# Sigmoid attention and a split-float16 feed-forward on one core: four decoded weight groups used by two batches, a third batch's attention in float32, and one sigmoid over two PSUM banks

## The chip, the cores and the metric

The kernel runs on one core of one Trainium2 chip. The time is the device time of one execution in microseconds (us). The kernel before took 1580.22 us, the median of three runs (1577.51 to 1587.48). A core has a matrix engine (TensorE, PE in the profile; its weight loads are PEld), a vector engine (VectorE, DVE), an activation engine (ScalarE, ACT), GpSimd (POOL), and a queue that here issues every DMA (SyncE, SP). Working memory is SBUF; matrix products land in PSUM, eight banks of 512 float32 numbers per partition.

## The reference

```python
def _attn_ref(q, k, v):                       # q, k, v: (8 batches, 12 heads, 448, 64), float32
    scores = scale * np.matmul(q, k.transpose(0, 1, 3, 2)) - np.log(S)
    attn = 1.0 / (1.0 + np.exp(-scores))
    return np.matmul(attn, v).astype(np.float32)

def _moe_ref(x, U, V, w_ch1, w_ch2):          # x: attention, heads side by side, (8, 448, 768)
    xt = x.transpose(0, 2, 1)
    h = xt @ U @ V                            # rank 32 over the 448 positions
    u = x + h.transpose(0, 2, 1)
    ch = np.maximum(u @ w_ch1, 0.0) @ w_ch2   # 768 -> 3072 -> 768
    return (u + ch).astype(np.float32)
```

U, V, w_ch1 and w_ch2 are float64; q, k and v are float32.

## The kernel before

Everything of a batch is kept with its 768 channels on partitions: six blocks of 128 channels by 448 positions, called u (`ua`, `ub` with a number in the profile). The heads go in six pairs.

**Attention** (`pair`, line 518). For batches 0 and 1 (`b < WHOLE`, WHOLE = 2) the scores and the products with the values are float32 matmuls straight from the loaded q, k and v (lines 495, 506, 510). For batches 2 to 7 each operand is scaled and split into a float16 high and a float16 low part, and three float16 products stand for one float32 product. This needs, for each pair, the largest magnitudes of q, k and v (`bound` on ACT, line 415), a scale through a DMA round trip (`scale_by_dma`), the high parts on POOL and the low parts on DVE, and the same split of the sigmoids (ACT line 603, DVE line 362, function `rest`). A pair has four blocks of key positions, of 128, 128, 128 and 64 (block 3 comes first); the two heads of a block go to two PSUM banks and are read by two sigmoids of 448 elements a partition each (line 582), eight in a pair.

**Mixing** (`mix`, `mix_half`): the rank-32 product over positions, added to u. Batches 1 to 7 are then parked in DRAM. For batches 0 to 3 `u_parts` splits u into float16 parts `us` (tiles us__86 and us__87).

**Feed-forward, batches 0 to 3** (`ffn_in`, line 830, `ffn_out`, line 850). The 3072 hidden channels come in six groups of 512. A group is 4 chains of 18 matmuls (768 inputs, three split products) and 6 chains of 12 matmuls: 144 matmuls of 128x448, float16. Each chain into the hidden layer is read by two ACT relus and one DVE subtraction (lines 837 to 839), each chain out of it is added to u on DVE (line 857; shown as line 362).

**Decoding** (`decode`, line 772). While batch 0 runs, each group's two weight matrices are loaded as raw float64 words (`w<-w_in`), in four pieces of 768 columns each. A piece takes three integer operations on DVE (`to_f32`: one on line 359, two on line 362), the largest magnitude on ACT (line 415), then, once the scale of all four pieces has gone through a small PE transpose (line 377), the high part on ACT and the low part on DVE (line 362). The finished pair goes to a two-deep ring (`w__88` to `w__91`) and to DRAM (`scratch`). Batches 1 to 3 load each group again from `scratch` (`fetch`).

**Batches 4 to 7** run the feed-forward in pairs of batches with seven block products in place of eight (`in_quad`, `out_quad`; all their matmuls are line 1025), after sums of weight quarters (`quarter_sums`) and of u blocks (`far_forms`, `near_forms`) have been formed.

**Order.** Nothing is ordered by a scheduler on the chip or by the framework: each operation is recorded in `Plan` with a rough cost and a position (`pos`), and a list scheduler in the kernel file walks the engines, takes the operation that can start first, the lowest position among several, and so fixes one instruction order for each engine. Positions come from the table of numbers on lines 59 to 67 (START, BEFORE, PREP and so on). On the chip each engine then works its list in that order, and an instruction that waits holds up everything behind it on its engine. The feed-forward slots of batches 0 to 3 are 24, `slots = [(b, g) for b in range(PLAIN) for g in range(NG)]` (line 1145): six groups of batch 0, six of batch 1, and so on; the attention of batch 1 is placed among batch 0's slots, that of batches 2 to 7 (in the order `LATER`) among the slots of batches 1 to 3.

Of the kernel before, what the change touches and what calls it, by code (L numbers as in the profile page):

```python
# [37 lines left out]
P = 128  # L38
D = 64
# [25 lines left out]
U_AT, U_STEP = 4.779, 5.064
LEAD, SUMS, STEP_K, STEP_I, FFN_LEAD = 28.26, 19.594, 38.128, 13.566, 4.0
# [22 lines left out]
class Plan:  # L89
# [36 lines left out]
    def order(self):  # L126
# [19 lines left out]
        def room(i):  # L146

            when, taken = 0.0, []
            for t in self.ops[i][7]:
                if t.got is None:  # L150
# [3 lines left out]
                    for b in t.buffers:  # L154
                        if b.live or b in taken or any(x.live for x in b.shares):
# [65 lines left out]
def fused_kernel(ctx: ExitStack, tc: tile.TileContext, q, k, v, wu, wv, w1, w2, out):  # L221
# [20 lines left out]
    puv = buf("puv", [1], F32)  # L242
# [12 lines left out]
    a_, at_ = buf("a", [14 * S], F32), buf("at", [5 * S], F32)  # L255
    A2, A1 = [Buffer(a_[:, 2 * i * S : 2 * (i + 1) * S]) for i in range(6)], [Buffer(a_[:, i * S : (i + 1) * S]) for i in (12, 13)]
# [39 lines left out]
    BANK = [Buffer(ps.tile([P, 512], F32, name=f"bank{i}")) for i in range(8)]  # L296
# [29 lines left out]
    FAR = {n: [Buffer(dram.tile([P, n], F32, name=f"far{n}_{i}")) for i in range(3)] for n in (3,)}  # L326
# [95 lines left out]

    FFN = 6 * (4 * 18 + 6 * 12) * MM
    BEGIN = [START]
    for b in range(PLAIN):
        BEGIN.append(BEGIN[-1] + FFN + (ROOM0 if not b else ROOM * len(LATER) / (PLAIN - 1)))

# [50 lines left out]
    def scores_of(b, js, products, kp, pos, early):  # L478


        sc = {(j, h): plan.tile("sc", BANK if early else PS_[b], False) for j in js for h in range(2)}
        n = 1 if b < WHOLE else 3

        def fn():
            for j in js:
                for i, (x, y) in enumerate(products()):
                    for h in range(2):
                        if b < WHOLE:
                            o = sc[j, h].x[:, :S] if j < 3 else sc[j, h].x[rows_of(h), :S]
                            keys = x[rows_of(h), j * P : min(S, j * P + P)]  # L490
                        else:
                            o = sc[j, h].x[:, :S]
                            first = j * P - (D if j == 3 and h else 0)
                            keys = x[rows_of(h), first : first + P]
                        nc.tensor.matmul(o, keys, y[rows_of(h)], start=i == 0, stop=i == n - 1)  # L495

        scored.append(pe(len(js) * (4 if b < WHOLE else 3) * MM + 0.2, fn, kp, list(sc.values()), pos, after=values_ops[-2:-1]))
        return sc

    def values_of(b, products, tiles, kp, pos):  # L500
# [14 lines left out]
        values_ops.append(pe((16 if b < WHOLE else 12) * MM + 0.2, fn, kp, [av], pos))  # L515
        return av

    def pair(b, p, at, d):
        whole = b < WHOLE
# [16 lines left out]
        else:  # L536
            prep = at - PREP
            st, ss = plan.tile("stg", STG), sm("ss", 3)
            for i in range(2):
                bound(lambda i=i: qk.x[:, i, :], S, lambda i=i: ss.x[:, i : i + 1], kqk[2 * i : 2 * i + 2], (ss, i), prep - BOUNDS, 0.73)  # L540
            bound(lambda: v32.x.rearrange("p a b -> p (a b)"), 512, lambda: ss.x[:, 2:3], [v32], (ss, 2), prep - BOUNDS, 0.82)
            s, inv = scale_by_dma(ss, [(ss, i) for i in range(3)], 3, "qkv", prep - BOUNDS + 1)
            cc, cv = sm("c", 1), sm("cv", 1)
            pool(0.5, lambda: ts(nc.gpsimd, cc.x, inv.x[:, 0:1], inv.x[:, 1:2], ALU.mult, 1.0 / math.sqrt(D), ALU.mult), [inv], [cc], prep + 1)
            pool(0.45, lambda: ts(nc.gpsimd, cv.x, inv.x[:, 2:3], 1.0 / A_UP, ALU.mult, 1.0, ALU.mult), [inv], [cv], prep + 1)
# [14 lines left out]
            pool(0.8, lambda: scaled(part(4), v32.x, s.x[:, 2:3]), [v32, s], [(st, 4)], prep + 6, plan.wrote["decoded"])  # L560
            dve2(0.75, lambda: rest(part(5), v32.x, s.x[:, 2:3], part(4)), [v32, s, (st, 4)], [(st, 5)], prep + 7)
# [17 lines left out]
            c, kc = cc, [cc]  # L579

        def sigmoid(cost, out_, in_, rows, pos, kin, kout):
            act(cost, lambda: nc.scalar.activation(  # L582
                out_(), in_(), AF.Sigmoid, bias=bias_s[rows], scale=c if whole else c.x[rows]), kin + ["bias"] + kc, kout, pos)

        sc = {}
        for n, j in enumerate((3, 0, 1, 2)):
# [6 lines left out]
            to = a if whole else plan.tile(*(("t1", AT1) if j == 3 else ("t2", AT2)))  # L593
# [692 lines left out]
```

## Time and profile before

| what | value |
|---|---|
| median of 3 runs | 1580.22 us |
| lowest and highest run | 1577.51, 1587.48 us |
| span of the profiled execution | 1577.4 us |
| busy PE, DVE, ACT, POOL | 98%, 71%, 54%, 23% |
| PE's first matmul after the span's start | 4.2 us |
| first feed-forward matmul | 83.7 us |
| mean granted TensorE clock | 0.996 |

The profiled execution's span, 1577.4 us, lies 0.1 us under the lowest of the three runs, and 2.8 us under their median. A row of a timeline has the start, the busy time, the engine, the line, the operation with output and inputs, their shapes, and the number of instructions merged into it; in brackets stand the idle time before it and what ended that. A matmul is pipelined, so its row's busy time is longer than its place in the stream: the price of a run of matmuls is read from its start to the next row's start. A float32 matmul appears as two records. In a row of windows stand, for each engine, busy time and number of instructions, then the granted clock (PEclk), the DMA share and GB/s.

### The profile page before, as it was taken

Reading aid. Unit: us, or ns where it says so; the run is one execution under the profiler, and the core shown is the slowest. Engines: PE = TensorE matmul, PEld = TensorE weight load, DVE = VectorE, ACT = ScalarE, POOL = GpSimd, SP = SyncE. Lnnn points to the kernel's source line nnn. Section 1 sums busy time; section 2 is a strip of 40 time slices with the busy share of each in tenths; the row PEclk is TensorE's granted clock in tenths of the full one; section 3 lists DMA queues with packets and bytes.
Section 4 is the critical chain, followed back from the end, with each engine's and each line's share of the span. In section 5 each row is a group of like instructions: output and inputs, shape, how many; then the busy total and the mean of one; then the engine's idle time right before and its main releaser. Section 6 shows DMA issues by size and latency. Waiting matters only on the chain.

```text
span 1577.4 us, 23653 instructions
## 1 busy us (share of the span) xinstructions
PE 1551.6 (98%) x8711; PEld 763.4 (48%) x8711; DVE 1125.1 (71%) x1886; ACT 854.6 (54%) x1521; POOL 355.7 (23%) x465
## 2 busy tenths in 40 slices
PE   8999989999999999999999999999999999999999
PEld 3344444544444444444444454455555555555554
DVE  3898889757776867667666777578768677565656
ACT  6756655468867766867867758342323524121210
POOL 0200002452212344211163410044554310000000
PEclk9999999999999999999999999999999999999999
DMA  8788988886576887664765684987576664233321
GB/s 250 249 296 275 295 276 259 301 237 162 148 215 162 196 255 230 189 184 131 199 189 173 189 246 156 283 268 230 182 222 204 242 209 165 105 106 137 109 106 70
DMA packets 208723, 319.36 MB, mean 202 GB/s; under 512 B 126176, under 2 KB 174688, under 8 KB 196320
## 3 DMA queue, kind: packets, MB, share of 16 engines
q1 hardware_dynamic: 208608, 317.86, 64.6%
q8 instruction: 68, 1.11, 0.3%
q14 instruction: 47, 0.39, 0.1%
HBM read 246.25 MB, written 77.42 MB: 205 GB/s over the span
## 4 chain that ended last, share of the span: by engine, by line
PE 93%; DMA 2%; DVE 2%; ACT 1%; SPq 1%; issue 0%; ACTq 0%; DVEq 0%
PE bank L1025 36%; PE bank L830 20%; PE bank L850 19%; PE bank L495 8%; PE bank L510 6%; PE bank L506 2%; DMA qk__100<-k_in 1%; PE bank L747 1%; DMA qk__98<-q_in 0%; PE bank L756 0%; PE bank L666 0%; SPq L339 0%; DVE stg__107 L362 0%; PE bank L654 0%; PE bank L691 0%
## 5 line engine op out<-in xcount | busy, mean ns | idle before, releaser
L850 PE MATMUL bank<-h__92,w__90 128*128 128x448 f16 x864 | 172.7, 353 | 0.8 <-DVE ua__76 L362 0.8
L850 PE MATMUL bank<-h__93,w__91 128*128 128x448 f16 x864 | 170.7, 353 | 0.4 <-DVE e_w__187 L380 0.4
L362 DVE SCALAR_TENSOR_TENSOR a<-at,a 128x896 f16<-128x896 f32 (+1 forms) x144 | 145.2, 1020 | 27.7 <-ACT a L603 26.9
L830 PEld LDWEIGHTS <-w__88 128*128 128x128 f16 x864 | 84.1, 98 | 86.4 <-issue 11.3
L830 PEld LDWEIGHTS <-w__89 128*128 128x128 f16 x864 | 83.8, 99 | 86.7 <-issue 13.2
L850 PEld LDWEIGHTS <-w__90 128*128 128x128 f16 x864 | 81.7, 98 | 87.0 <-issue 14.3
L603 ACT ACTIVATE a<-at 128x896 f16<-128x896 f32 (+1 forms) x144 | 122.9, 854 | 0.7
L850 PEld LDWEIGHTS <-w__91 128*128 128x128 f16 x864 | 82.5, 98 | 83.9 <-issue 10.4
L1025 PEld LDWEIGHTS <-w__88 128*128 128x128 f16 x756 | 73.8, 98 | 72.8 <-issue 4.1
L1025 PEld LDWEIGHTS <-w__90 128*128 128x128 f16 x756 | 74.0, 98 | 69.0
L1025 PEld LDWEIGHTS <-w__91 128*128 128x128 f16 x756 | 74.0, 98 | 68.9
L1025 PEld LDWEIGHTS <-w__89 128*128 128x128 f16 x756 | 74.0, 98 | 68.9
L913 POOL TENSOR_TENSOR w<-w 128x384 f32<-128x384 f32 x96 | 103.8, 1082 | 5.0
L830 PE MATMUL bank<-us__86,w__89 128*128 128x448 f16 x432 | 86.6, 357 | 4.0 <-DVE ua__79 L362 3.4
L830 PE MATMUL bank<-us__86,w__88 128*128 128x448 f16 x432 | 85.7, 357 | 3.7 <-DVE ua__74 L362 3.7
L830 PE MATMUL bank<-us__87,w__88 128*128 128x448 f16 x432 | 85.5, 353 | 0.3 <-ACT r__94 L837 0.3
L830 PE MATMUL bank<-us__87,w__89 128*128 128x448 f16 x432 | 85.8, 353 | 0.0
L582 ACT ACTIVATE at<-bank,bias_s,c__223 128x448 f32<-128x448 f32 (+1 forms) x96 | 66.5, 722 | 21.3 <-PE bank L495 17.2
L909 POOL TENSOR_TENSOR w<-w 128x384 f32<-128x384 f16 x48 | 45.6, 974 | 119.1 <-DVE xnt L917 76.5
L582 ACT ACTIVATE at<-bank,bias_s,c__222 128x448 f32<-128x448 f32 (+1 forms) x96 | 66.8, 721 | 8.2 <-PE bank L495 6.3
L582 ACT ACTIVATE at<-bank,bias_s,c__221 128x448 f32<-128x448 f32 (+1 forms) x96 | 66.9, 722 | 7.1 <-PE bank L495 6.4
L909 POOL TENSOR_TENSOR w<-w__88 128x384 f32<-128x384 f16 x16 | 14.9, 952 | 209.2 <-DVE stg__108 L362 185.8
(1195 smaller groups left out, 3097.7 us busy)
## 6 DMA issues: line engine op xcount, KB each, us to landing
w<-w_in SPq DMA_DIRECT2D x48, 768.0 KB, 6.0
forms<-xnt SPq DMA_DIRECT2D x24, 768.0 KB, 4.3
w__88<-forms SPq DMA_DIRECT2D x12, 1344.0 KB, 5.7
w__89<-forms SPq DMA_DIRECT2D x12, 1344.0 KB, 5.8
w__90<-forms SPq DMA_DIRECT2D x12, 1344.0 KB, 6.0
w__91<-forms SPq DMA_DIRECT2D x12, 1344.0 KB, 6.1
forms<-scratch SPq DMA_DIRECT2D x144, 96.0 KB, 4.2
w__88<-scratch SPq DMA_DIRECT2D x9, 1536.0 KB, 8.5
```

The lines of the kernel that those rows point to most:

```text
L362: nc.vector.scalar_tensor_tensor(out=out, in0=in0, scalar=s, in1=in1, op0=op0, op1=op1)
L495: nc.tensor.matmul(o, keys, y[rows_of(h)], start=i == 0, stop=i == n - 1)
L506: nc.tensor.matmul(av.x[:, :S], x[:, 3, :], y(tiles[3], 0), start=i == 0, stop=False, skip_group_check=True)
L510: nc.tensor.matmul(av.x[rows_of(h), :S], x[:, j, rows_of(h)], y(tiles[j], h), start=False, stop=j == 2 and i == n - 1, skip_group_check=True,)
L582: act(cost, lambda: nc.scalar.activation(out_(), in_(), AF.Sigmoid, bias=bias_s[rows], scale=c if whole else c.x[rows]), kin + ["bias"] + ...
L603: act(0.57 if j == 3 else 0.95, lambda a=a, to=to: nc.scalar.activation(half(a, 0), to.x, AF.Copy, scale=A_UP), kto, [(a, 0)], here + A_OFF)
L747: nc.tensor.matmul(tp.x[:, :384], m.rearrange("p a b -> p (a b)"), x[:, j], start=j == 0, stop=j == 6)
L830: nc.tensor.matmul(ph.x[:, :S], wx[:, x, c, f * P : (f + 1) * P], us.x[:, c, y, :], start=c == 0 and i == 0, stop=c == NP - 1 and i == 2,)
L850: nc.tensor.matmul(po.x[:, :S], wx[:, x, f, e * P : (e + 1) * P], h.x[:, f, y, :], start=f == 0 and i == 0, stop=f == FC - 1 and i == 2,)
L909: pool(1.0, lambda j=j: nc.gpsimd.tensor_tensor(out=t.x[:, j], in0=quarter(j, 0), in1=quarter(j, 1), op=ALU.add), [(w, j, 0), (w, j, 1)] i ...
L913: pool(1.0, lambda o_=o_, x=x, y=y, sub=sub: nc.gpsimd.tensor_tensor(out=t.x[:, o_], in0=t.x[:, x], in1=t.x[:, y], op=ALU.subtract if sub ...
L1025: nc.tensor.matmul(bank.x[:, :S], wt.x[:, k, FACTOR[n], x], both(f)[:, y], start=start and k == i == 0, stop=k == 2 and i == 2, skip_group ...
```

## The change

- **Slots.** The list of slots becomes (0,0), (0,1), then for groups 2 to 5 (`TOGETHER`) batch 0 and at once batch 1 with the same decoded weights in the ring; batch 1's groups 0 and 1 follow, fetched from `scratch`, then batches 2 and 3 as before. Batch 1's attention is placed before the end of group 1, it isn't parked, and stays in the `ub` blocks. kg, the factor of each group for batches 0 and 1, is made group by group.
- **Batch 2.** WHOLE goes from 2 to 3: batch 2's scores and values are float32 matmuls, without bounds, scales and splits. It and the later batches get six u blocks of their own (`UC`), and batch 2's attention is placed in the stage of decoding.
- **Sigmoids.** PSUM is laid out as four tiles of two banks. The two heads of key blocks 0 to 2 go to the two halves of one tile and one sigmoid of 2 x 448 elements reads both; block 3's two heads share one bank (64 rows each) and take one sigmoid of 448. A pair has four sigmoids in place of eight.
- **Room.** To pay for the u blocks: value blocks 4 to 2, two-head sigmoid blocks 6 to 5, and the many small tiles are columns of one tile `tiny`. Temporaries of decoded pieces from group 2 on no longer use us__87's place. The table of positions is new.

The diff, cut:

```diff
-WHOLE = 2
+WHOLE = 3
-LATER = [2, 4, 3, 5, 6, 7]
+LATER = [4, 3, 5, 6, 7]
+TOGETHER = (2, 3, 4, 5)
-START, DECODE = 47.709, 44.285
+START, DECODE = 53.869, 35.813
...
-    UA, UB = ring("ua", NP, [S], F32), ring("ub", NP, [S], F32)
+    UA, UB, UC = (ring(f"u{x}", NP, [S], F32) for x in "abc")
...
-    V32 = ring("v", 4, [4, P], F32)
+    V32 = ring("v", 2, [4, P], F32)
...
-    BANK = [Buffer(ps.tile([P, 512], F32, name=f"bank{i}")) for i in range(8)]
+    BANK, TWO = [], []
+    for i in range(4):
+        t = ps.tile([P, 1024], F32, name=f"banks{i}")
+        BANK += [Buffer(t[:, :512]), Buffer(t[:, 512:])]
+        TWO.append(Buffer(t.rearrange("p (h s) -> p h s", h=2)))
...
+    slots = [(0, 0), (0, 1)]
+    for g in range(2, NG):
+        slots += [(0, g)] + [(1, g)] * (g in TOGETHER)
+    first_pass = len(slots)
+    slots += [(1, g) for g in range(NG) if g not in TOGETHER]
+    slots += [(b, g) for b in range(2, PLAIN) for g in range(NG)]
...
-        sc = {(j, h): plan.tile("sc", BANK if early else PS_[b], False) for j in js for h in range(2)}
+        sc = {}
+        for j in js:
+            if j < 3:
+                sc[j] = plan.tile("sc2", TWO if early else TWO[2:], False)
+            else:
+                sc[j] = plan.tile("sc", BANK if early else PS_[b][:3] if b >= 2 else PS_[b], False)
...
-            for h in range(2):
-                rows = rows_of(h) if j == 3 else slice(0, P)
-                cols = slice(0, S) if j == 3 else slice(h * S, h * S + S)
-                sigmoid(0.66 if whole else 0.72, lambda to=to, rows=rows, cols=cols: to.x[rows, cols],
-                        lambda h=h, sc=sc, j=j, rows=rows: sc[j, h].x[rows, :S], rows, here, [sc[j, h]], [(to, h)])
+            if j == 3:
+                sigmoid(0.66 if whole else 0.72, lambda to=to: to.x, lambda sc=sc: sc[3].x[:, :S], [sc[3]], [to], here)
+            else:
+                sigmoid(1.13 if whole else 1.19, lambda to=to: to.x.rearrange("p (h s) -> p h s", h=2), lambda sc=sc, j=j: sc[j].x[:, :, :S], [sc[j]], [to], here)
...
             if b == 0:
                 decode(i, g, at + i * step / 2 - DECODE)
+            elif n < first_pass:
+                ws[i, b, g] = ws[i, 0, g]
             else:
                 fetch(i, b, g, at - step + i * step / 2)
```

**Where the instructions stand.** Three places. The first is PE where, among the chains out of batch 0's group 2, the next slot begins. Before, a chain out of the hidden layer (weights w__90) and a pair's values are followed by group 3 of batch 0 (us__86 with w__89):

```order
L850 MATMUL bank_109<-h__92,w__90 128x448
L506 MATMUL bank_116<-a,v__104 128x448
L510 MATMUL bank_116<-a,v__104 64x448 x6
L830 LDWEIGHTS w__89
L830 MATMUL bank_110<-us__86,w__89 128x448
```

Now the next slot is the same group's first weights (w__91, the tile that batch 0 has just used) with batch 1's u (us__90):

```order
L881 MATMUL banks_111<-h__95,w__93 128x448
L520 MATMUL banks_112<-qk__102 64x448 x2
L520 MATMUL banks_113<-qk__102 128x448 x2
L531 MATMUL banks_112<-a,v__104 128x448
L535 MATMUL banks_112<-a,v__104 64x448 x6
L861 LDWEIGHTS w__91
L861 MATMUL banks_110<-us__90,w__91 128x448
```

What moved: 144 matmuls of batch 1 stand between two groups of batch 0, so twice as much of PE's work lies between the ends of two decoded groups. The attention before this point is the pair work of batch 2 here (float32, from qk).

The second is DVE in the same stage, behind the low parts of a group's second weights. Before (group 4; w__90 is written), between the integer operations on the next pieces (us__87<-w) stands batch 0 alone:

```order
L362 SCALAR_TENSOR_TENSOR w__90<-stg__107,s_w__191,w__90 128x768 x2
L362 SCALAR_TENSOR_TENSOR w__90<-stg__108,s_w__191,w__90 128x768 x2
L359 TENSOR_SCALAR p_72<-p_72 128x1
L839 TENSOR_TENSOR h__92<-r__95,h__92 128x448
L807 TENSOR_TENSOR kg__176<-inv_u__170,p_72 128x1
L362 SCALAR_TENSOR_TENSOR us__87<-w_106,us__87 128x768
```

Now (group 3; w__94), the chains of batch 1 (ub) are added between the pieces as well:

```order
L381 SCALAR_TENSOR_TENSOR w__94<-stg__109,tiny,w__94 128x768 x2
L870 TENSOR_TENSOR h__95<-r__98,h__95 128x448
L378 TENSOR_SCALAR stg__108<-w_107 128x768 x2
L381 SCALAR_TENSOR_TENSOR stg__108<-w_107,stg__108 128x768 x4
L381 SCALAR_TENSOR_TENSOR ub__78<-banks_110,tiny,ub__78 128x448
L438 TENSOR_REDUCE tiny<-uc__84 128x1
L378 TENSOR_SCALAR stg__109<-w_107 128x768
```

What moved: six additions and four subtractions of batch 1 join each of groups 2 to 5 on DVE, and batch 2's largest values (uc) come here.

The third is DVE before the first feed-forward chain, which needs all low parts of batch 0's u. Before, these stand ahead of the low parts of group 0's second weights:

```order
L362 SCALAR_TENSOR_TENSOR us__86<-ua__78,s_u__173,us__86 128x448
L362 SCALAR_TENSOR_TENSOR us__86<-ua__79,s_u__173,us__86 128x448
L362 SCALAR_TENSOR_TENSOR w__90<-at,s_w__192,w__90 128x768 x2
L362 SCALAR_TENSOR_TENSOR w__90<-us__87,s_w__192,w__90 128x768 x2
L362 SCALAR_TENSOR_TENSOR stg__107<-w_106,stg__107 128x768
```

Now they stand behind them and behind two operations on the next pieces:

```order
L381 SCALAR_TENSOR_TENSOR w__93<-us__90,tiny,w__93 128x768
L378 TENSOR_SCALAR tiny<-tiny 128x1
L381 SCALAR_TENSOR_TENSOR us__90<-w_107,us__90 128x768
L403 RECIPROCAL tiny<-tiny 128x1
L378 TENSOR_SCALAR stg__108<-w_107 128x768
L755 TENSOR_TENSOR tiny<-tiny 128x1
L483 COPY vraw<-ua 64x128
L381 SCALAR_TENSOR_TENSOR us__89<-ua__71,tiny,us__89 128x448
L381 SCALAR_TENSOR_TENSOR us__89<-ua__72,tiny,us__89 128x448
```

What moved: four low parts of weights and two operations on pieces from behind the six low parts of u to ahead of them.

More of the change, by code (lines that the diff above doesn't have):

```diff
@@ L420, in largest @@
             kx, [ko], pos)
[L423 to L426, printed above, removed]
+    slots = [(0, 0), (0, 1)]
[4 more added lines that the diff above has]
+    slots += [(b, g) for b in range(2, PLAIN) for g in range(NG)]
+    GROUP = (4 * 18 + 6 * 12) * MM
+    AT = [START]
+    for n in range(len(slots)):
+        AT.append(AT[-1] + GROUP + (ROOM0 / first_pass if n < first_pass else ROOM * len(LATER) / (len(slots) - first_pass)))
+    BEGIN = [AT[slots.index((b, 0))] for b in range(PLAIN)] + [AT[-1]]
+    MIDDLE = AT[first_pass]
     def mixing():
@@ L487, in fn @@
                     for h in range(2):
[L488 to L497, printed above, removed]
+                        o = sc[j].x[:, h, :S] if j < 3 else sc[j].x[rows_of(h), :S]
+                        nc.tensor.matmul(o, x[rows_of(h), j * P : min(S, j * P + P)], y[rows_of(h)], start=i == 0, stop=i == n - 1)
+        scored.append(pe(len(js) * (4 if b < WHOLE else 3) * MM + 0.2, fn, kp, list(sc.values()), pos, after=values_ops[-2:-1] + scored[-1:]))
         return sc
@@ L579, in pair, with value_products, sigmoid @@
             c, kc = cc, [cc]
-        def sigmoid(cost, out_, in_, rows, pos, kin, kout):
+            if direct:
+                kvalue = [v32]
+                def value_products():
+                    return [(v32.x, lambda t, h: t.x[:, h * S : (h + 1) * S])]
+        def sigmoid(cost, out_, in_, kin, kout, pos):
             act(cost, lambda: nc.scalar.activation(
-                out_(), in_(), AF.Sigmoid, bias=bias_s[rows], scale=c if whole else c.x[rows]), kin + ["bias"] + kc, kout, pos)
+                out_(), in_(), AF.Sigmoid, bias=bias_s, scale=c if whole else c.x), kin + ["bias"] + kc, kout, pos)
         sc = {}
@@ L620, in new_u @@
     def new_u(b):
-        u32s[b] = [plan.tile(f"u{'ab'[b > 0]}{c}", [(UB if b else UA)[c]]) for c in range(NP)]
+        u32s[b] = [plan.tile(f"u{'abc'[min(b, 2)]}{c}", [(UA, UB, UC)[min(b, 2)][c]]) for c in range(NP)]
         mxs[b] = sm("mx", NP) if b < PLAIN else sm(f"mx{b}", NP, 1)
@@ L1144, in fused_kernel @@
     PATTERN = "ioiooioioo"
-    slots = [(b, g) for b in range(PLAIN) for g in range(NG)]
     entered = []
     def units(n):
-        b = min(n // NG, PLAIN - 1)
-        step = (BEGIN[b + 1] - BEGIN[b]) / NG
-        at = BEGIN[b] + (n - b * NG) * step
         nf = ne = 0
+        at = AT[min(n, len(slots))]
+        step = AT[min(n, len(slots) - 1) + 1] - AT[min(n, len(slots) - 1)]
+        banks = PF[0] if n < first_pass else PF[1]
         for x in PATTERN:
@@ L1156, in units @@
                 if n < len(slots):
-                    ffn_in(*slots[n], nf, at)
+                    ffn_in(*slots[n], nf, at, banks)
                 nf += 1
@@ L1161, in units @@
                 if n:
-                    ffn_out(*slots[n - 1], ne, at)
+                    ffn_out(*slots[n - 1], ne, at, banks)
                 ne += 1
```

137 lines of the change are left out of this document (76 added, 61 removed).

## The prediction

> **What bounds the kernel now.** I read the busy times first, then the windows (busy time by stage), then PE's waits, and last the timeline around them.
>
> ```profile
> PE 1551.6 (98%) x8711; PEld 763.4 (48%) x8711; DVE 1125.1 (71%) x1886; ACT 854.6 (54%) x1521; POOL 355.7 (23%) x465
> ```
>
> 98% alone proves little, since a pipelined matmul's row is longer than its place in the stream. The windows tell more:
>
> ```profile
> 80.00:120.00 40.00, 40.00 (x198) 18.40 (x198) 37.59 (x64) 24.17 (x45) 0.00 (x0) 0.97 0.89 299
> 160.00:200.00 40.00, 36.55 (x179) 16.60 (x177) 33.80 (x61) 25.49 (x52) 0.00 (x0) 0.96 0.89 289
> 200.00:240.00 40.00, 35.91 (x183) 18.20 (x182) 36.17 (x65) 22.18 (x42) 0.00 (x0) 0.96 0.82 272
> 240.00:280.00 40.00, 36.22 (x194) 19.63 (x193) 36.97 (x72) 21.03 (x39) 8.77 (x11) 0.96 0.80 250
> 400.00:500.00 100.00, 100.00 (x632) 48.36 (x631) 72.99 (x128) 74.33 (x133) 24.23 (x40) 1.00 0.58 157
> 1400.00:1500.00 100.00, 100.00 (x531) 51.71 (x529) 59.20 (x98) 24.84 (x44) 0.00 (x0) 1.00 0.31 111
> ```
>
> From 1400 to 1500 us PE sends 531 matmuls in 100 us, one each 188 ns. The same spacing is in the feed-forward amid attention:
>
> ```profile
> 307.51 6.98 PE L830 MATMUL bank<-us__87,w__88 128*128 128x448 f16 x36
> 314.33 3.57 PE L830 MATMUL bank<-us__87,w__89 128*128 128x448 f16 x18
> 317.83 1.31 PE L495 MATMUL bank<-stg__108 64*128 64x448 f16 x12
> 319.07 2.44 PE L850 MATMUL bank<-h__92,w__90 128*128 128x448 f16 x12
> 321.36 0.73 PE L506 MATMUL bank<-a,stg__107 128*128 128x448 f16 x3
> 322.02 1.89 PE L510 MATMUL bank<-a,stg__107 128*64 128x448 f16 x18
> 323.84 3.58 PE L830 MATMUL bank<-us__87,w__89 128*128 128x448 f16 x18
> ```
>
> 36 take 6.82 us from start to start, 189 ns each. The next 18 take 3.50 instead of 3.41: about 0.09 us goes at a switch into attention matmuls that use half the array. So from 300 us on PE is a full stream. The exceptions are earlier, above all between 160 and 280 us, where PE is idle at times and DVE is busy 34 to 37 of 40 us. The longest, apart from the load at the start:
>
> ```profile
> PE bank L830 <- DVE ua__74 L362: 3.7, 1, 3.7
> PE bank L830 <- DVE ua__79 L362: 3.4, 1, 3.4
> PE bank L676 <- ACT xnt L669: 2.3, 1, 2.3
> PE bank L506 <- ACT a L582: 2.2, 1, 2.2
> PE bank L1025 <- DMA stg__107<-ufar: 2.0, 1, 2.0
> PE bank L676 <- DVE xnt L362: 1.4, 1, 1.4
> ```
>
> The two longest wait for DVE to add a finished chain to batch 0's u, which gives the PSUM bank back. DVE does so late (ua__79, at 188.15), because it works its list in order and decoding stands ahead:
>
> ```profile
> 187.21 0.16 DVE L766 TENSOR_REDUCE mm_w__183<-ssw__180 128x1 f32<-128x4 f32 x1 [1.04 <-ACT junk L415]
> 187.28 0.95 DVE L362 SCALAR_TENSOR_TENSOR us__87<-w,us__87 128x768 int32<-128x768 int32 x1
> 188.15 0.68 DVE L362 SCALAR_TENSOR_TENSOR ua__79<-bank,kg__176,ua__79 128x448 f32<-128x448 f32 x1
> ```
>
> **The change part by part.** *The third batch in float32* is PE work that is added to a full stream. One float32 pair, from starts to next starts:
>
> ```profile
> 97.55 1.77 PE L495 MATMUL bank<-qk__100 64*128 64x448 f32 x8
> 99.25 9.26 PE L850 MATMUL bank<-h__92,w__90 128*128 128x448 f16 x48
> 108.44 1.92 PE L495 MATMUL bank<-qk__98 64*64 64x448 f32 x8
> 110.29 1.02 PE L506 MATMUL bank<-a,v__101 128*128 128x448 f32 x2
> 111.24 2.48 PE L510 MATMUL bank<-a,v__101 128*64 128x448 f32 x12
> 113.65 0.32 PE L377 MATMUL bank<-ident,mm_w__182 128*128 128x128 f32 x1
> ```
>
> 1.70 + 1.85 for the scores, 0.95 + 2.41 for the values: 6.91 us. In float16 it is two score blocks of 1.24 (317.83 to 319.07), then 0.66 + 1.82 (321.36, 322.02, 323.84): 4.96 us. Six pairs cost 6 x 1.95 = 11.7 us. The order has 130 switches into attention where it had 119: 11 x 0.09 = 1.0 us. Added: 12.7 us. Everything else on PE keeps its count.
>
> *Four groups for two batches.* A piece of weights costs DVE one operation of line 359 and two of line 362 on integers, and a low part. The groups' means:
>
> ```profile
> L362 DVE SCALAR_TENSOR_TENSOR us__87<-w,us__87 128x768 int32<-128x768 int32 x30 | 28.5, 954 | 0.1
> L359 DVE TENSOR_SCALAR us__87<-w 128x768 int32<-128x768 int32 x15 | 8.3, 554 | 1.0 <-DMA w<-w_in 1.0
> L362 DVE SCALAR_TENSOR_TENSOR ua__74<-bank,kg__176,ua__74 128x448 f32<-128x448 f32 x12 | 8.2, 681 | 6.6 <-PE bank L850 6.4
> L839 DVE TENSOR_TENSOR h__93<-r__94,h__93 128x448 f16<-128x448 f32 x24 | 14.9, 620 | 1.6 <-ACT r__94 L837 1.3 <-ACT h__93 L838 0.2
> ```
>
> A low part is 0.95 us (the rows of w__88 and w__91 below). A group's eight pieces are 8 x (0.55 + 1.91 + 0.95) = 27.3 us of DVE; a slot's chains are 6 x 0.68 + 4 x 0.62 = 6.6 us. Before: 33.9 us of DVE to a slot with 144 x 0.189 = 27.2 us of PE, and only batch 1's attention to fill the gap. Now, for groups 2 to 5: 40.5 us of DVE to 54.4 us of PE. DVE falls from over PE to well under it.
>
> What is late next? For groups 0 and 1 nothing is doubled, and batch 1's mixing comes before group 2's end. So I added up both lists, each row at the mean of its kind. The list before holds 117 us of DVE work up to the low parts of group 2's first weights and 261 us up to those of group 5's second; the profile has their ends, and the first chain:
>
> ```profile
> 140.49 1.95 DVE L362 SCALAR_TENSOR_TENSOR w__88<-stg__107,s_w__192,w__88 128x768 f16<-128x768 f32 x2
> 276.72 1.00 DVE L362 SCALAR_TENSOR_TENSOR w__91<-stg__108,s_w__193,w__91 128x768 f16<-128x768 f32 x1
> 83.72 13.79 PE L830 MATMUL bank<-us__86,w__88 128*128 128x448 f16 x72
> ```
>
> 142.4 and 277.7: DVE's pace is 135 us to 144 of such work, 0.94. The changed list has 119, 166, 183 and 204 us up to group 2's first weights, batch 1's u, and group 3's first and second weights: ready at 144, 189, 204 and 224 us. PE's list by its spacings puts the chains that need them at 146, 192, 214 and 256, and the first chain came 9 us behind that reckoning (75 by the list, 83.7 in the row): 155, 201, 223 and 265. After group 1 there is no place where DVE is behind, and the slack grows from 11 to 41 us.
>
> So the waits on DVE and ACT from 160 to 280 us should go: 3.7 + 3.4 + 2.3 + 1.4 = 10.8 us. With them goes the lower clock that follows each: granted clock 0.96 in three windows of 40 us is 3 x 0.04 x 40 = 4.8 us. Together 15.6 us, the upper bound of this stage's gain; the lower bound is nothing, if each wait finds a successor. I take 14: mixing is still a chain between PE, ACT and DVE, and some of its 3.7 us may stay.
>
> *First chain.* Before, PE waits just ahead of it (2.2 us, ACT, and a clock of 0.97 in the window 80:120, 1.2 us). Now u's low parts stand behind 4 x 0.95 us of weights and 0.95 + 0.55 of pieces on DVE, 5.3 us, and PE's list has 1.6 us more attention ahead of the chain. Between 0 and +3.7 us; I take 0, since those four low parts are then done ahead of what follows.
>
> *Sigmoids.* No row shows one over two banks.
>
> ```profile
> L582 ACT ACTIVATE at<-bank,bias_s,c__221 128x448 f32<-128x448 f32 x72 | 49.7, 724 | 2.9 <-PE bank L495 2.4
> L603 ACT ACTIVATE a<-at 128x896 f16<-128x896 f32 x108 | 102.6, 950 | 0.6
> L603 ACT ACTIVATE a<-at 128x448 f16<-128x448 f32 x36 | 20.3, 565 | 0.0
> ```
>
> At most it costs two of 0.72 (1.45 us), at least 0.72 plus the 0.39 that a copy's second 448 elements cost (1.11 us). I take the latter, it is the same engine at the same size. ACT gains at least nothing and at most 3 x 0.34 + 0.72 = 1.7 us a pair, but ACT is busy 74 of 100 us where PE is full: 0 on the path. The price is that the first bank is given back 0.39 us later (third rival).
>
> *DMA and room.* Eight of 36 fetches of weights and batch 1's parking fall away, at most 9 us of transfer each:
>
> ```profile
> w__88<-scratch SPq DMA_DIRECT2D x9, 1536.0 KB, 8.5
> ```
>
> PE waited for none of them, so 0; if a fetch were on the path, 8.5 us would be its price. Fewer value and sigmoid blocks act on batches 3 to 7; the five batches have the time that six had less the two slots moved, about as long per pair, so 0, covered by the 25 us in 100 that ACT and DVE have free.
>
> Sum, on the profiled execution: 1577.4 + 12.7 - 14.0 = 1576.1 us. The span holds all of its own time but 0.1 us; the runs' median is 2.8 above the profiled one, and I add half of that, since one run in three is as fast: **1577 us**. What the first stage gives, the float32 batch takes.
>
> **The skill's other reading.** By the Trainium skill (Perfetto Trace Analysis, section Identifying the Most-Contended Engine), matmul busy time doesn't tell how near PE is to its limit; the busy share of weight loads does. That is 48% here, and would leave PE room for the float32 work at no cost. The trace disagrees: weight loads are busy 51.71 of 100 us where matmuls follow each other at 188 ns without a wait.
>
> **The rivals.** (1) *DVE stays the limit of decoding.* The waits move to groups 0 to 2 and mixing, nothing is won: 1577.4 + 12.7 = 1590.1, about +0.8%. For it: at group 0 the low parts of u come later, and two batches' additions queue on one DVE. The change would then not do what it is built for. Against it: 40.5 us of DVE to 54.4 of PE.
>
> (2) *Everything is won*, also the waits outside decoding (2.2 + 2.0) and the clock of 80:120 (1.2): 1590.1 - 15.6 - 5.4 = 1569.1, -0.5%. For it: DVE's slack grows as counted. Against it: first chain and the step to line 1025 are not made easier.
>
> (3) *The two-bank sigmoid holds PSUM*, and the kernel is slower. From batch 3 on, two score blocks need four banks free at once out of five, and each comes back 0.39 to 0.72 us later. If PE comes for them less than that after they are free, each of 30 pairs' three sigmoids stalls it: 90 x 0.39 = 35 us, and 1576.1 + 35 = 1611, +2%; from 17 us of such stalls on it is slower by over 1%. For it: no row shows how PE fares when two banks come back together. Against it: the list above has no wait of 1.4 us or more between 300 and 1000 us, though today's score blocks need four of five banks too.
>
> (4) *PE is not the bound*, and float32 is free: 1577.4 - 15.6 = 1561.8, -1.0%. For it speaks 48%; against it the stream at 188 ns.
>
> **How the numbers follow.** Forecast 0.68; (1) 0.14; (2) 0.05; (3) 0.10; (4) 0.03. The forecast's own range is 1570 to 1584, from a gain between 8 and 15.6, the first chain's +3.7, and 2.8 for the run. To leave out no more than 2 in 10, the range takes in (1) and (2): 1566 to 1593. A measurement of this kernel can tell about 1% from no change. Faster by over 1% is (4) and a tail of (2): 0.04. Slower by over 1% is (3) and a tail of (1): 0.12. Within 1%: 0.84.
>
> **What would show it.** Right: PE's waits for ua additions and for xnt gone, clock 1.00 from 160 to 300 us, first-stage DVE below 35 of 40 us; float32 pairs of batch 2 at 6.9 us; a two-bank sigmoid near 1.1 us; PE's sum longer by 12.7 us. Wrong: new waits of PE on ACT L615 (PSUM) after 400 us, on DVE before 200 us, or a float32 pair that costs PE no more than 5 us.

## The result, and the profile after

The changed kernel takes **1640.76 us** (median of 4 runs, 1636.70 to 1644.29) where the kernel before takes 1581.24 (4 runs beside it). The ratio is 1.0379, with a 95% interval of 1.0349 to 1.0409: slower by 3.8%, and 48 us above the end of the predicted range. The profiled execution has a span of 1642.5 us. All ratios below are of fast runs; one slow run, among the five of the groups alone (2060.65 us at a granted clock of 0.75), is not in its ratio.

First the busy times of the changed kernel, then its windows (the columns as in the prediction: PE, PEld, DVE, ACT, POOL, each with its instructions, then clock, DMA share, GB/s):

```profile
PE 1581.4 (96%) x8621; PEld 761.8 (46%) x8621; DVE 1089.9 (66%) x1831; ACT 753.2 (46%) x1269; POOL 349.3 (21%) x429
```

```profile
160.00:200.00 40.00, 39.27 (x210) 19.82 (x209) 33.07 (x66) 18.29 (x33) 2.65 (x3) 1.00 0.74 207
200.00:240.00 40.00, 39.02 (x199) 18.18 (x198) 33.30 (x60) 23.14 (x40) 0.31 (x1) 1.00 0.84 258
240.00:280.00 40.00, 40.00 (x201) 18.24 (x200) 25.21 (x40) 18.55 (x33) 0.00 (x0) 1.00 0.66 212
...
500.00:600.00 100.00, 95.98 (x564) 46.53 (x563) 57.50 (x93) 46.10 (x76) 44.01 (x56) 0.98 0.70 199
600.00:700.00 100.00, 90.25 (x548) 41.80 (x547) 62.84 (x105) 62.34 (x104) 17.70 (x29) 0.97 0.65 180
...
1000.00:1100.00 100.00, 90.68 (x489) 43.71 (x490) 70.39 (x119) 41.67 (x67) 14.47 (x16) 0.95 0.72 221
...
1400.00:1500.00 100.00, 99.00 (x523) 50.90 (x522) 58.87 (x98) 24.05 (x43) 0.00 (x0) 1.00 0.33 117
```

The stage that the prediction was about went as it said: from 160 to 280 us PE's gaps are almost closed (118.3 of 120 us instead of 108.7), the clock is 1.00 and DVE is busy 33, 33 and 25 of 40 us. The loss lies where the prediction expected nothing. From 400 us on PE is no full stream any more: no window of 100 us has it busy for all of its length. Even from 1400 to 1500 us, where batches 4 to 7 go through their quarter products, which the change is not about, PE sends 523 instead of 531. No other engine is near its limit there.

PE's waits (engine, line, what it waited for; us in total, times, longest) have turned from a few long ones into many short ones. The rows of the list add up to 57.0 us in 55 waits, against 21.9 us in 13 before. Its head:

```profile
PE banks L520 <- DMA qk__101<-q_in: 4.2, 1, 4.2
PE banks L1056 <- DVE us__90 L381: 3.7, 1, 3.7
PE banks L881 <- ACT at L615: 3.3, 2, 2.1
PE banks L520 <- ACT at L615: 3.1, 2, 1.9
...
PE banks L396 <- ACT r__98 L868: 2.4, 1, 2.4
```

L520 are the scores, L881 the feed-forward chains out of the hidden layer (L861 those into it), L396 the transposes of scales, L1056 the quarter products, L381 DVE's additions, L868 a relu. Of these five, every row but the first waits for an instruction that reads PSUM, and the partners look odd: in the third a feed-forward chain waits for a sigmoid, in the last a small transpose waits for a relu. From the third batch on, feed-forward chains use banks 0 to 2 and score blocks banks 3 to 7, so they share no bank; but banks 2 and 3 now share a tile.

The program itself says why. Each wait in it names an instruction, and that instruction's operands can be laid beside those of the waiting one. In the kernel before, 3 of PE's some 980 waits on ACT and DVE name an instruction whose bytes the waiting matmul doesn't touch. In the changed kernel 312 (145 on ACT, 167 on DVE) name one that touches only the **other** half of the `banks` tile that the matmul writes, which is another bank. The framework orders accesses by tile, and the tiles now hold two banks. Readers have the same: 219 waits of ACT and DVE (73 and 146) name a matmul that writes the neighbouring bank, so that a finished chain is read only when the chain beside it is finished too. (Below, a false wait is one of PE's that names only the neighbouring bank; the price of one is the whole loss divided by their number, so what the readers' false waits cost is in it.)

### The profile page after: what moved, and what is told of

Its sections match the earlier page's. It is cut to its first block, busy times and chain, and to the rows that moved or that the text cites. A ratio compares the mean times of both kernels' runs of the same rounds, so it can differ in the third digit from the quotient of the medians.

```text
span 1642.5 us, 23045 instructions
## 1 busy us (share of the span) xinstructions
PE 1581.4 (96%) x8621; PEld 761.8 (46%) x8621; DVE 1089.9 (66%) x1831; ACT 753.2 (46%) x1269; POOL 349.3 (21%) x429
## 4 chain that ended last, share of the span: by engine, by line
PE 84%; DVE 7%; ACT 3%; DMA 3%; SPq 1%; issue 1%; ACTq 0%; DVEq 0%
PE banks L1056 31%; PE banks L881 18%; PE banks L861 18%; PE banks L520 7%; PE banks L535 5%; PE banks L531 2%; DVE stg__108 L381 1%; DMA w<-w_in 1%; PE banks L779 1%; SPq L771 1%; ACT at L615 1%; DVE a L381 0%; DMA w<-parked 0%; DVE w L381 0%; DMA at<-ufar 0%
## 5 line engine op out<-in xcount | busy, mean ns | idle before, releaser
L881 PE MATMUL banks<-h__95,w__93 128*128 128x448 f16 x720 | 145.3, 355 | 6.3 <-ACT h__96 L869 2.5
L881 PE MATMUL banks<-h__96,w__94 128*128 128x448 f16 x720 | 146.6, 356 | 3.8 <-ACT h__95 L869 1.4
L381 DVE SCALAR_TENSOR_TENSOR a<-at,a 128x448 f16<-128x448 f32 (+1 forms) x120 | 120.0, 1024 | 24.8 <-ACT a L635 24.6
L615 ACT ACTIVATE at<-banks,tiny 128x448 f32<-128x448 f32 (+1 forms) x120 | 115.7, 1003 | 39.9 <-DVE a L381 13.6
L881 PEld LDWEIGHTS <-w__93 128*128 128x128 f16 x864 | 82.9, 98 | 93.4 <-issue 21.2
L881 PEld LDWEIGHTS <-w__94 128*128 128x128 f16 x864 | 82.6, 99 | 91.2 <-issue 20.3
L861 PEld LDWEIGHTS <-w__92 128*128 128x128 f16 x864 | 83.5, 98 | 89.0 <-issue 14.5
L861 PEld LDWEIGHTS <-w__91 128*128 128x128 f16 x864 | 83.6, 98 | 84.4 <-issue 8.9
L1056 PEld LDWEIGHTS <-w__91 128*128 128x128 f16 x819 | 80.1, 98 | 82.6 <-issue 5.4
L1056 PEld LDWEIGHTS <-w__93 128*128 128x128 f16 x756 | 74.7, 99 | 79.0 <-issue 12.3
L1056 PEld LDWEIGHTS <-w__92 128*128 128x128 f16 x756 | 73.9, 98 | 72.3 <-issue 3.7
L378 POOL TENSOR_SCALAR tiny<-tiny 128x1 f32<-128x1 f32 (+1 forms) x90 | 26.7, 307 | 345.0 <-DVE tiny L378 332.2
L1056 PEld LDWEIGHTS <-w__94 128*128 128x128 f16 x693 | 67.6, 98 | 68.5 <-issue 3.3
L635 ACT ACTIVATE a<-at 128x448 f16<-128x448 f32 (+1 forms) x120 | 97.6, 856 | 1.4 <-PE banks L535 1.1
L861 PE MATMUL banks<-us__89,w__92 128*128 128x448 f16 x432 | 86.9, 356 | 2.8 <-ACT h__96 L869 1.1
L861 PE MATMUL banks<-us__90,w__92 128*128 128x448 f16 x432 | 85.6, 353 | 1.7 <-ACT h__96 L869 1.6
L861 PE MATMUL banks<-us__90,w__91 128*128 128x448 f16 x432 | 85.1, 353 | 2.0 <-DVE tiny L399 1.0
L861 PE MATMUL banks<-us__89,w__91 128*128 128x448 f16 x432 | 85.5, 353 | 0.1
L615 ACT ACTIVATE a<-banks,tiny 128x448 f32<-128x448 f32 (+1 forms) x72 | 62.6, 911 | 27.2 <-PE banks L535 18.5
L868 ACT ACTIVATE r__98<-banks 128x448 f32<-128x448 f32 x48 | 26.0, 541 | 75.7 <-PE banks L861 43.4
```

The costliest lines, as they stand in the source:

```text
L378: eng.tensor_scalar(out=out, in0=in_, scalar1=s1, scalar2=s2, op0=op0, **kw)
L381: nc.vector.scalar_tensor_tensor(out=out, in0=in0, scalar=s, in1=in1, op0=op0, op1=op1)
L615: act(cost, lambda: nc.scalar.activation(out_(), in_(), AF.Sigmoid, bias=bias_s, scale=c if whole else c.x), kin + ["bias"] + kc, kout, pos)
L635: act(0.57 if j == 3 else 0.95, lambda a=a, to=to: nc.scalar.activation(half(a, 0), to.x, AF.Copy, scale=A_UP), kto, [(a, 0)], here + A_OFF)
L861: nc.tensor.matmul(ph.x[:, :S], wx[:, x, c, f * P : (f + 1) * P], us.x[:, c, y, :], start=c == 0 and i == 0, stop=c == NP - 1 and i == 2,)
L881: nc.tensor.matmul(po.x[:, :S], wx[:, x, f, e * P : (e + 1) * P], h.x[:, f, y, :], start=f == 0 and i == 0, stop=f == FC - 1 and i == 2,)
```

## Experiments

Four explanations were to be told apart. A: these waits between the two banks of a tile. B: the prediction's third rival, the merged sigmoid holds PSUM longer. C: the new order, or fewer buffers (A2 from 6 to 5, V32 from 4 to 2). D: float32 in the third batch is dearer than priced.

### The kernel before, with tiles of two banks

```diff
-    BANK = [Buffer(ps.tile([P, 512], F32, name=f"bank{i}")) for i in range(8)]
+    BANK = []
+    for i in range(4):
+        t = ps.tile([P, 1024], F32, name=f"banks{i}")
+        BANK += [Buffer(t[:, :512]), Buffer(t[:, 512:])]
```

> The kernel before, with one edit: the eight PSUM banks come from four tiles of two banks each, as in the change, instead of eight tiles of one bank. Every instruction and every engine's order are those of before; only the waits that the framework derives from tiles differ. Counted in the built program, 415 of PE's waits on ACT and DVE (before: 3; changed kernel: 312) now name an instruction that touches only the neighbouring bank of the tile. Theory A (waits between the two banks of a tile): the changed kernel's 53 us of added stalls are 0.17 us for each of its 312, so 415 cost about 70 us: near 1650 us, 1615 to 1690. Theory B (the merged sigmoid holds PSUM longer): none is merged here, so 1581 within 0.5%. Theory C (new order, fewer buffers) and theory D (float32 of the third batch dearer than priced): 1581 within 0.5%.

Measured: 1670.76 us, ratio 1.0587 (1.0562 to 1.0611). The order of every engine is that of before, no sigmoid is merged, no batch is in float32, no buffer is smaller, and the kernel is 90 us slower. B, C and D cannot make that. The window that was a full stream with 531 matmuls before:

```profile
1400.00:1500.00 100.00, 97.80 (x517) 50.21 (x515) 61.45 (x103) 27.37 (x51) 0.00 (x0) 1.00 0.32 112
```

### The change with one bank to a tile

```diff
-        t = ps.tile([P, 1024], F32, name=f"banks{i}")
-        BANK += [Buffer(t[:, :512]), Buffer(t[:, 512:])]
-        TWO.append(Buffer(t.rearrange("p (h s) -> p h s", h=2)))
+        t = [ps.tile([P, 512], F32, name=f"bank{2 * i + h}") for h in range(2)]
+        BANK += [Buffer(x) for x in t]
+        TWO.append(Buffer(t))
...
-                sigmoid(1.13 if whole else 1.19, ..., sc[j].x[:, :, :S], [sc[j]], [to], here)
+                two_sigmoids(1.13 if whole else 1.19, to, sc[j], here)
```

`two_sigmoids` issues one sigmoid per head and bank, at the place of the merged one.

> The changed kernel with eight tiles of one bank each; a score block's two heads then have a sigmoid each, issued one behind the other where the merged one stood. All else, and the order on every engine, is that of the change. No wait between banks is left. Theory A: the added stalls go, PE's sum stays: 1641 - 53 = 1588 us, 1573 to 1595. Theory B: the same, since nothing is merged any more. Theories C and D: it stays at 1641 within 1%.

Measured: 1581.65 us, ratio 1.0005 (0.9990 to 1.0020). All of the loss is gone: 59.1 us. The quarter products are a full stream again:

```profile
1400.00:1500.00 100.00, 100.00 (x530) 51.76 (x529) 59.74 (x99) 24.36 (x44) 0.00 (x0) 1.00 0.32 112
```

PE's waits are now 11.7 us in 10; the longest (L1064 is L1056 of the change, L889 its L881):

```profile
PE bank L520 <- DMA qk__101<-q_in: 4.3, 1, 4.3
PE bank L1064 <- DMA v__104<-ufar: 2.5, 1, 2.5
PE bank L1064 <- DMA at<-ufar: 2.2, 3, 1.2
PE bank L889 <- ACT h__95 L877: 1.2, 1, 1.2
```

What one wait looks like is best seen where the two kernels run the same rows in the same order. First the changed kernel's timeline (start, duration, engine, line, operation, in brackets the idle time before and what ended it):

```profile
1498.71 0.68 DVE L381 SCALAR_TENSOR_TENSOR us__89<-banks,tiny,us__89 128x448 f32<-128x448 f32 x1
...
1500.06 0.73 PE L1056 MATMUL banks<-uc__85,w__94 128*128 128x448 f16 x3
1500.26 0.69 DVE L381 SCALAR_TENSOR_TENSOR ub__81<-banks,tiny,ub__81 128x448 f32<-128x448 f32 x1 [0.88 <-PE banks L1056]
1500.63 0.73 PE L1056 MATMUL banks<-w,w__94 128*128 128x448 f16 x3
...
1501.20 0.73 PE L1056 MATMUL banks<-uc__83,w__94 128*128 128x448 f16 x3
1501.40 0.68 DVE L381 SCALAR_TENSOR_TENSOR ub__81<-banks,tiny,ub__81 128x448 f32<-128x448 f32 x1
1501.99 0.68 DVE L381 SCALAR_TENSOR_TENSOR ua__72<-banks,tiny,ua__72 128x448 f32<-128x448 f32 x1
...
1502.72 0.54 PE L1056 MATMUL banks<-w,w__92 128*128 128x448 f16 x2 [0.79 <-DVE ua__72 L381]
```

Then the same place in the change with single tiles:

```profile
1437.27 0.68 DVE L381 SCALAR_TENSOR_TENSOR us__89<-bank,tiny,us__89 128x448 f32<-128x448 f32 x1
...
1437.86 0.68 DVE L381 SCALAR_TENSOR_TENSOR ub__81<-bank,tiny,ub__81 128x448 f32<-128x448 f32 x1
...
1438.99 0.68 DVE L381 SCALAR_TENSOR_TENSOR ub__81<-bank,tiny,ub__81 128x448 f32<-128x448 f32 x1
...
1439.73 0.68 DVE L381 SCALAR_TENSOR_TENSOR ua__72<-bank,tiny,ua__72 128x448 f32<-128x448 f32 x1
...
1440.67 0.73 PE L1064 MATMUL bank<-uc__83,w__94 128*128 128x448 f16 x3
1441.23 0.73 PE L1064 MATMUL bank<-w,w__92 128*128 128x448 f16 x3
```

With single tiles three matmuls follow three by 0.56 us (1440.67, 1441.23). With pairs it is 1.52 us from 1501.20 to 1502.72: 0.96 us are lost, twice over by the same rule. The waiting matmul writes the lower half of `banks0`; by the program, its wait names the addition to ua__72, which reads the upper half and ends at 1502.67. The lower half's own reader, the first addition to ub__81, had ended at 1500.95, before PE came. And the addition is late because the first one for ub__81, which reads the lower half, stood 0.88 us waiting for the chain in the upper half; with single tiles it begins 0.59 us after us__89's addition began, at once after it.

The list of waits doesn't hold all of the loss. The two profiled spans differ by 64.6 us (1642.5 and 1577.9), the lists by 45.3 (57.0 and 11.7); the other 19 us are inside PE's busy time (1581.4 and 1562.5 us). Two things put them there. Of the 0.96 us above, 0.17 lie under the tail of the row before the wait (0.73 us long, 0.56 to the next); for 45 more waits that makes about 8 us, an estimate. And the granted clock is 0.98, 0.97, 0.98 and 0.95 in the windows that begin at 500, 600, 800 and 1000 us, where single tiles have 1.00: by an estimate 0.12 x 100 = 12 us, less the 2 of the one window in which single tiles have the lower clock (0.98 from 900 us).

### Pairs kept, merged sigmoid undone; and half the pairs undone

The first of these two differs from the run with single tiles in one thing, the tiles: it has the four two-bank tiles of the change, and `two_sigmoids`. The two programs have the same instructions in the same order on every engine, at the same PSUM addresses; the waits are what differs. The second has single tiles for banks 0 to 3 and pairs, with the merged sigmoid, for banks 4 to 7.

```diff
+        if i < 2:
+            t = [ps.tile([P, 512], F32, name=f"bank{2 * i + h}") for h in range(2)]
+            BANK += [Buffer(x) for x in t]
+            TWO.append(Buffer(t))
+        else:
...
```

> The changed kernel with its four two-bank tiles, but with two sigmoids per score block, one per bank, in the place of the merged one. Against the run with eight single tiles the instructions and their order are the same on every engine; only the tiles of PSUM differ. 400 of PE's waits name the neighbouring bank. Theory A: not faster than the change, 1640 to 1665 us. Theory B: the merged sigmoid is gone, so 1588 us, 1575 to 1600. Theories C and D: 1641 within 1%, and then the run with single tiles is 1641 too.

> The changed kernel with single tiles for banks 0 to 3 (feed-forward chains, value blocks, the quarter products) and two-bank tiles for banks 4 to 7, where 69 of the... score blocks' sigmoids stay merged (all but those of the first pairs that lie in banks 0 to 3). 103 of PE's waits name the neighbouring bank. Theory A: 103 x 0.17 = 18 us over the run with single tiles: about 1605 us, 1590 to 1620. Theory B: the merged sigmoids from batch 1 on are all there, so 1635 to 1641. Theories C and D: 1641 within 1%.

Measured: 1645.95 us (ratio 1.0427, 1.0401 to 1.0453) with the pairs and no merged sigmoid; 1598.34 us (1.0125, 1.0088 to 1.0161) with half the pairs. In the latter 129 of the 144 two-bank score blocks keep the merged sigmoid; the 69 in the expectation is a slip.

So B falls: without any merged sigmoid the loss stays whole (64.3 us over the run with single tiles), and with nine tenths of them it is 16.7 us. The count of waits tells it well: 64.3 us / 400 is 0.161 us for each, and 103 of them would make 16.6 us, where 16.7 were found. That it fits to 0.1 us is luck, since this run's interval is 6 us wide to each side and the price of a wait is not the same everywhere; but no part of the loss asks for the merging itself.

### Float32 alone, the groups alone, and four banks to a tile

The kernel before with `WHOLE = 3` (the third batch still mixed by halves); the change with single tiles and `WHOLE = 2`, its third batch in float16 again; the kernel before with `ps.tile([P, 2048], ...)`, four banks to a tile.

> The kernel before with the third batch's attention in float32 and nothing else (WHOLE 3, its mixing still by halves): single PSUM tiles, order made anew by the same planner. Priced on PE at 6 pairs x 1.95 us + a few switches = 12 to 13 us on a full stream: 1593 us, 1589 to 1598 (ratio 1.005 to 1.011). If PE were not the bound (the fourth rival of the prediction), float32 is free: 1581 within 0.3%. If float32 is dearer than priced (theory D): over 1600.

> The changed kernel with eight single PSUM tiles, a sigmoid per head, and the third batch's attention back in float16: what is left of the change is the four groups that serve two batches while decoded, the order that goes with them, the u blocks and the small tiles in one. If the decoding stage gives 14 us and the rest nothing, as priced: 1581.5 - 12.7 = 1569 us, 1564 to 1574. If the new order gave nothing and the run with single tiles was even with before by something else: 1580 or more.

> The kernel before with PSUM from two tiles of four banks each; instructions and orders as before. 524 of PE's waits on ACT and DVE now name an instruction in another bank of the tile. At the price of the two-bank run, 90 us / 415 = 0.22 us each, 524 give 114 us: 1695. It may be more, since with four banks in a tile the wait falls on a bank whose reader came later: 1680 to 1800. If the waits between banks were not the cause of the two-bank run's loss, 1671 or less.

Measured: 1579.52 us with float32 alone (ratio 0.9988, 0.9976 to 1.0000), 1624.43 us with the groups alone (1.0261, 1.0243 to 1.0279), 2022.6 us with four banks to a tile (1.2783, 1.2751 to 1.2815). All three leading expectations (1593, 1569 and 1695 us) were missed; float32 alone came out where its expectation put the case that PE is not the bound (1581 within 0.3%).

Four banks to a tile cost 441 us with 524 such waits, 0.84 us each: the sign is A's, the size is four times what the price of a pair gave. The list of PE's waits tells where it comes from: 319 waits with four banks to a tile (362.5 us), 71 with two (88.2 us). Each is about as long, 1.1 and 1.2 us on average; in more of them PE really stands idle.

*Float32 alone is free*, but not since PE has room all along: from 280 to 900 us its gaps are 1.0 us in all, 1.3 before. Its windows show where it was paid for:

```profile
160.00:200.00 40.00, 38.37 (x195) 17.80 (x194) 36.31 (x65) 25.86 (x48) 0.00 (x0) 1.00 0.89 302
200.00:240.00 40.00, 39.73 (x202) 19.19 (x201) 36.73 (x66) 26.25 (x50) 0.00 (x0) 1.00 0.92 305
240.00:280.00 40.00, 38.39 (x210) 20.20 (x209) 37.47 (x72) 21.54 (x38) 9.00 (x8) 1.00 0.76 258
```

The decoding stage has lost most of its gaps and its low clock, though no group was moved and DVE is as busy as before. Three float32 score blocks of the third batch begin at 209, 220 and 221 us there; in the kernel before that batch begins at 302.

*The groups alone* close the decoding stage too, and pay elsewhere:

```profile
160.00:200.00 40.00, 39.05 (x212) 20.59 (x211) 36.55 (x74) 15.64 (x29) 3.69 (x6) 1.00 0.83 224
200.00:240.00 40.00, 40.00 (x214) 20.86 (x213) 35.41 (x63) 20.46 (x38) 0.00 (x0) 1.00 0.86 276
240.00:280.00 40.00, 40.00 (x214) 20.88 (x213) 33.09 (x58) 18.43 (x34) 0.00 (x0) 1.00 0.63 231
480.00:520.00 40.00, 16.00 (x84) 5.79 (x79) 24.22 (x41) 16.08 (x30) 22.47 (x25) 0.62 0.74 198
```

Float16 staging may not begin before the last decoded weights are sent off (the `plan.wrote["decoded"]` of `pair`), so the third batch's scores start at 340 us instead of 179 (the change with single tiles). But with four groups moved ahead, only two slots stand between the decoding stage and that batch's first feed-forward. Its u is late; PE's longest wait is for mixing (L796):

```profile
PE bank L796 <- DVE xnt L381: 14.6, 4, 10.3
```

The run says nothing about the groups with a placing made for float16; it does say that the change's two halves need each other.

### Float32 alone, held back

Is the float32 batch free because it fills gaps? One edit on the float32 run, in `scores_of`:

```diff
-        scored.append(pe(..., list(sc.values()), pos, after=values_ops[-2:-1]))
+        scored.append(pe(..., list(sc.values()), pos, after=values_ops[-2:-1] + (plan.wrote["decoded"] if b == 2 else [])))
```

> The kernel before with the third batch in float32, as in the run before it, and one edit more: that batch's score blocks may not start before the last decoded weights have been sent to DRAM, which is the bar its float16 staging already has. In the run without the bar three score blocks, a pair and a half, ran at 209 to 221 us, in the decoding stage. Theory F (float32 attention was free there because it needs no staging on DVE and POOL, so the order draws it into PE's gaps of the decoding stage): now the gaps of 160 to 280 us come back, 18 us of stalls instead of 7, and the price of 12 us shows: 1590 us, 1586 to 1595, ratio 1.004 to 1.009. Theory G (float32 is free since PE has room, or the gaps close for another reason, less work on DVE): 1579.5 within 0.3%.

Measured: 1583.47 us, ratio 1.0025 (1.0013 to 1.0037). By the number that is still theory G's (up to 1584), short of F's 1586; but with the batch's first score block at 285 us one window opened again, as F had it, and two did not:

```profile
160.00:200.00 40.00, 38.37 (x195) 17.81 (x193) 36.56 (x65) 25.42 (x48) 0.00 (x0) 1.00 0.90 304
200.00:240.00 40.00, 35.91 (x183) 18.25 (x181) 36.34 (x66) 19.69 (x36) 0.00 (x0) 0.96 0.90 303
240.00:280.00 40.00, 39.55 (x218) 21.20 (x217) 39.43 (x72) 20.37 (x35) 9.25 (x8) 1.00 0.86 279
```

So filling gaps is worth 4 to 6 us, in the window in which the three blocks stood (1583.47 - 1579.52 is 4.0; the ratios differ by 0.0037, which is 5.8; their intervals don't meet). That is the smaller part of what should have been a price of 12. The other two windows have 1.8 and 3.3 us less of gaps than before and a clock of 1.00 for 0.96 (3.2 us), in an order made anew; which of its moves does it was not separated, and stays open.

## Why the prediction was wrong, point by point

**The step that failed** is the one on sigmoids and room. It priced the new sigmoid, wrote "0 on the path", and took the later return of the first bank as the only price of two banks together. The lines of the diff that make the sigmoid possible, eight PSUM tiles turned into four, got no term of their own. Their term is 59 us: 1640.76 with pairs, 1581.65 with single tiles, in the same order of instructions but for the sigmoids. What makes it up is not the sigmoid but the waits: 312 of PE's on ACT and DVE name only a neighbouring bank, 0.19 us of loss for each. The four rivals did not hold it either: the second (1569) and the fourth (1562, PE not the bound) lie below every run here, the first ends at 1590. The third named the right place, PSUM, and the nearest number (1611), but its mechanism, 90 blocks at 0.39 us, is refuted by the run without merged sigmoids. It would also have left the quarter products alone, where no sigmoid runs and PE loses 8 of 531 matmuls in 100 us. The sign that the prediction itself set down, new waits of PE on L615 after 400 us, did come, four times between 600 and 930 us, 6.4 us in all; the list shows them among waits on many other readers of PSUM.

A rule should have raised the question. The Trainium skill (PSUM — Partial Sum Buffer, section PSUM bank collisions raise a hardware error) says to guard PSUM by bank and quadrant, by bank in the simple version. The waits of the changed kernel guard more than that, two banks at once, and the runs give what the surplus costs: 0.16 us for each of 400 waits.

**PE as the bound** held. With single tiles PE's waits are half of those before, and the run lands at 1581.65 us, 4.7 above the forecast of 1577 and inside its own range of 1570 to 1584. What was forecast is that kernel. But that the sum fits is in part luck: two of its terms were off by about as much in opposite directions, as the next two points show.

**Float32 of the third batch, +11.7.** The price was right on PE. The third batch's first score blocks and values, in the change with single tiles:

```profile
185.93 1.77 PE L520 MATMUL bank<-qk__101 64*128 64x448 f32 x8
187.63 4.71 PE L889 MATMUL bank<-h__95,w__93 128*128 128x448 f16 x24
192.28 1.92 PE L520 MATMUL bank<-qk__102 64*64 64x448 f32 x8
194.13 1.02 PE L531 MATMUL bank<-a,v__104 128*128 128x448 f32 x2
195.08 2.48 PE L535 MATMUL bank<-a,v__104 128*64 128x448 f32 x12
197.49 6.98 PE L869 MATMUL bank<-us__90,w__91 128*128 128x448 f16 x36
```

One block of each kind, 1.70 + 1.85 + 0.95 + 2.41, is 6.91 us, as priced. Wrong was to add it to the decoding stage's gain as if the two were independent: float32 alone already won most of that gain (1579.52 us), so the groups' share on top of it is none that can be measured. Against 1581.71 + 12.7 us float32 alone is 15 us cheaper than its term, and the groups, added to it, bring nothing in place of 14.

**The decoding stage, -14.** Right in kind and size, for the changed kernel with single tiles:

```profile
160.00:200.00 40.00, 40.00 (x207) 18.78 (x206) 35.46 (x69) 19.06 (x35) 2.48 (x3) 1.00 0.77 208
200.00:240.00 40.00, 40.00 (x205) 18.93 (x204) 32.70 (x58) 25.57 (x48) 0.00 (x0) 1.00 0.84 276
240.00:280.00 40.00, 40.00 (x207) 19.34 (x206) 25.94 (x44) 18.49 (x36) 0.00 (x0) 1.00 0.68 221
```

11.3 us of gaps and three windows at clock 0.96 are gone. One sign was just missed, DVE below 35 of 40 us in the first window (35.46). The first rival (DVE stays the limit) is refuted. One reading on the way was a little low: by the rows of w__88 and w__91 a low part is 0.98 to 1.00 us, not 0.95, up to 0.4 us more to a group of eight, which changes no step.

**The first chain, 0, at most +3.7.** With single tiles it starts at 81.06 us, 2.7 earlier than before; with pairs at 87.39, 3.7 later. In the latter two score blocks just ahead of it wait for ACT:

```profile
84.33 1.02 PE L520 MATMUL banks<-qk__103 64*128 64x448 f32 x4 [1.63 <-ACT a L615]
86.43 1.02 PE L520 MATMUL banks<-qk__103 64*128 64x448 f32 x4 [1.08 <-ACT ub__78 L641]
87.39 3.58 PE L861 MATMUL banks<-us__89,w__91 128*128 128x448 f16 x18
```

The bound was met, by a cause that the step did not name: with single tiles neither wait is there.

**A sigmoid over two banks** takes what was said, and no run shows that it earned anything on the path:

```profile
L615 ACT ACTIVATE at<-banks,tiny 128x896 f32<-128x896 f32 x90 | 96.4, 1097 | 22.3 <-DVE a L381 13.6 <-PE banks L520 5.7 <-DVE ua__73 L381 2.4
```

1.10 us against the 1.11 taken. Merged rather than split, on the same tiles, is 1640.76 against 1645.95 us, with 88 fewer of the false waits, and the intervals of the two ratios overlap; the pairs that it needs cost 59.

**Fetches, parking and buffers, 0**, and the new order, 0 beyond the decoding stage: the run with single tiles has them all, and stands at 1.0005. That bears out their sum; that each is 0 was not shown. PE's waits on DMA at the quarter products, for one, are 4.7 us there instead of 2.7.

No version that beat both kernels came out of this: float32 alone, at 0.9988 with the interval touching 1, is the kernel before as far as this can tell.

## What to carry to other kernels

When a diff changes how on-chip memory is cut into tiles, count the waits that the framework draws from tiles before pricing anything else: whoever shares a tile waits for the other's reader, and the other's writer, even at other addresses. A wider instruction that needs a wider tile is worth it only if the engine it relieves is on the path. And where a gain and a cost of one change touch the same stage, run each alone; here the cost alone came out free.

## What the runs showed that had not been expected

- The price of one false wait is no constant: 0.16 to 0.22 us with two banks to a tile (64.3 us / 400; 89.8 us / 415), 0.84 us with four (441 us / 524), where the list of PE's waits has 319 instead of 71.
- A stream can lose 59 us in waits of which the longest on a reader of PSUM is 3.7 us and most are under 1, while PE stays busy 96% of the span and its busy time even grows by 30 us (1551.6 to 1581.4; 11 of them are there with single tiles too, 1562.5). Only the counts of matmuls in the windows (523 for 531) and the partners in the list of waits gave it away.
- The granted clock fell to 0.62 in the 40 us window in which PE was busy 16 us, and in the changed kernel to 0.95 to 0.98 in four of the five windows of 100 us that have 4 to 10 us of gaps; the fifth, from 900 us, has 4.2 us of gaps and a clock of 1.00.
